# An mLSTM layer with an MLP: the order of its first steps written anew, and the last unit stored in two halves

## Chip, cores and metric

The kernel runs on one core of one Trainium2 chip. The metric is the device time of one execution in microseconds (us). The core has five engines with queues of their own: TensorE (PE, its weight loads PEld), VectorE (DVE), ScalarE (ACT), GpSimd (POOL) and SyncE (SP), which here issues nearly all DMA transfers.

## What is computed

Batch 4, 8 heads, 768 tokens, head size 40; then an MLP over the 3072 tokens with model size 320 and hidden size 2048. The recurrence, per head, with `C` a 40x40 state and `n` a vector:

```
m_new = max(f_t + m, i_t);  fs = exp(f_t + m - m_new);  is = exp(i_t - m_new)
C = fs*C + is * v k^T;      n = fs*n + is*k
y = sigmoid(o) * (C q) / max(|n.q|, 1)
out = silu(x @ w_in) @ w_out        # x = y with the heads side by side
```

w_in and w_out come as 64-bit floats, all else as 32-bit; the output is 32-bit.

## The kernel before

**Tiling.** The tokens are 24 units: 6 chunks of 128 tokens by 4 batch rows, unit n being chunk n // 4. A unit runs through the attention (two half chunks of 64 tokens, 8 heads as two sets of 4), which ends in a transposed x split into a rounded high part and a low rest. The MLP runs in an opening over units 0 to 3 and then in steps 1 to 10 of two units each. Hidden columns come in 16 groups of 128 (fc); a step takes two groups at a time (s = 0 to 7).

**Order.** Nothing is scheduled by the compiler: `ORDER` is a long list of words, and each word is one small step that puts its instructions at the end of the queues of the engines concerned. Every engine works its own list in order and waits by semaphores. SyncE too: a DMA issue that waits holds all DMA issues behind it. `V` and `Q` (and some `S`) also put an empty instruction on SyncE that waits for their matmuls.

**The words of a unit n:** `qk`, `kvo`, `lq`, `d` are its loads (L470, L479, L502, L490); `s`, `sp`, `sb` build the exponents of the first four units in PSUM by matmul (L526, L551, L564); `e` the exponential; `S` scores (L668, 32 matmuls); `w` scores times weights on DVE (L687); `v` weighted values on DVE (L605); `P` products for the state (L632); `c` the carry of the state (ACT copy, POOL and DVE); `l` the exponential of lq (ACT, L614), `q` the scaled queries (POOL, L618); `V` values (L697); `Q` queries against the state (L716, 16 matmuls for units 0 to 3, otherwise 32); `g` normalisation and output gate (five DVE steps, L733 to L743); `x` the transpose (L753 to L756); `h`, `y` high and low part (ACT, DVE).

**The gates of chunk c:** `gs`, `gu`, `gm`, `gt` on DVE, `gf` six small matmuls and a copy, and `go` the store of the summed forget gates to a DRAM scratch `LFd` (L276), from which `lq` and `d` are read.

**Weights.** w_in comes in 8 blocks `i` of 256 columns (256 rows) and 2 blocks `c` (the last 64 rows for four `i` blocks, L317), w_out in 8 blocks `o`. `L` loads one (L314), `M` (ACT, L329), `S`, `Z`, `J` (DVE, L337, L344, L357) turn 64-bit floats into 32-bit, `T` and `R` (ACT L381, DVE L386) split w_in into high and low part.

**MLP.** In the opening `m`, `a`, `b`, `n` with a letter A (units 0, 1), B (2, 3) or J (all four) and fc: first product (L780), tanh (L826), gate (L831), second product (L842 to L845). In a step j, `m`, `a`, `b`, `f`, `F`, `n` with j.s; the second product is L918. `On` copies unit n from PSUM (L929), `Dn` stores it (L799).

**Spins.** `z7*10` is ten matmuls of 128x512 bf16 on a constant into bank 7 (L939); they compute nothing that is used. The kernel has 39 of them, all before 16 us.

Of the kernel before, what the change touches and what calls it, by code (L numbers as in the profile page):

```python
# [49 lines left out]
ORDER = """  # L50
Li0 Li1 gs0 z2*5 z7*6 z7*6 gu0 kvo1 z7*2 z7*2 s0 Mi1 gm0 gt0 kvo0 gs1 s1 Si1 sp1 t1 z2*5 Mi0 Si0 Zi0 Zi1 sb1 Lc0 sp0 sb0
e0 gu1 e1 z7*10 gm1 Ji0 Mc0 Ti0 z7*1 v0 go0 qk1 lq0 S1 Sc0 gt1 qk0 z7*2 s3 Ji1 lq1 P0 Li3 qk2 lq2 Zc0 sb3 v1 Jc0 w1 t0
l0 c0 Ri0 S0 Tc0 Ti1 w0 sp3 l1 P1 Rc0 V0 gf1 q0 kvo2 Q0 s2 g0 Mi3 qk3 sp2 Si3 V1 q1 c1 sb2 e3 Zi3 Q1 g1 kvo3 S2 x0 lq3
e2 x1 l2 h0 h1 v2 w2 P2 Lo0 y0 Ri1 Li2 y1 q2 Lo1 t2 Ji3 V2 go1 c2 Lo3 mA0 v3 Q2 g2 S3 Lo2 t3 l3 P3 w3 aA0 mA1 c3 V3 bA0
aA1 x2 q3 Mo0 bA1 Q3 So0 h2 mA3 Zo0 mA2 y2 Jo0 Li4 Ti3 nA0 g3 Lc4 x3 nA1 Ri3 Mi2 d4 aA3 Mo1 bA3 So1 h3 y3 d5 aA2 mB0 bA2
Zo1 Jo1 Mo3 aB0 Si2 mJ6 Mi4 aJ6 bB0 Zi2 Ji2 nA3 gs2 lq4 Ti2 bJ6 mB2 qk4 nA2 kvo4 aB2 bB2 k5.0 So3 k4.1 nB0 Ri2 Mc4 Zo3
Jo3 Mo2 Li5 mJ7 k4.0 aJ7 mJ4 nJ6 aJ4 So2 bJ7 lq5 Sc4 qk5 Zo2 Si4 e4.0 e4.1 nJ7 mB3 bJ4 l4 Li6 aB3 Zc4 nB2 Zi4 v4 Ji4 Ti4
q4 mJ5 Jo2 S4.0 Lo5 Jc4 Mi5 Tc4 Lo4 bB3 Si5 P4 S4.1 gu2 aJ5 d6 Zi5 Ji5 Ti5 bJ5 nJ4 mB1 nJ5 k5.1 Ri4 Rc4 gm2 aB1 bB1 mJ9
aJ9 Ri5 mJ8 w4 bJ9 kvo5 Mo5 c4 e5.0 Mi6 Lo6 Mo4 So4 nB1 Si6 qk6 V4 e5.1 gt2 aJ8 Zo4 Li7 k6.1 l5 S5.0 t4 mJ10 bJ8 S5.1
Jo4 Q4 Zi6 Ji6 So5 nB3 Ti6 k6.0 nJ9 g4 nJ8 Ri6 Zo5 go2 e6.1 Mi7 v5 aJ10 kvo6 Si7 d7 mJ12 w5 Mo6 bJ10 Zi7 aJ12 Ji7 P5 V5  # L60
Jo5 Lo7 S6.0 q5 mJ13 c5 t5 So6 Q5 S6.1 e6.0 gl k7.0 aJ13 nJ10 bJ12 v6 mJ11 lq6 Ti7 aJ11 w6 Zo6 Mo7 x4 Jo6 bJ13 lq8 lq7
d8 Ri7 g5 nJ12 mJ14 h4 P6 k8.0 V6 y4 k7.1 bJ11 l6 l7 gf2 kvo7 e7.0 d9 mJ15 x5 uh0 So7 kvo8 qk7 h5 ul0 t6 Zo7 uh1 aJ14 y5
Jo7 nJ11 bJ14 nJ13 aJ15 q6 m1.0 bJ15 a1.0 ul1 nJ14 nJ15 b1.0 c6 m1.3 e7.1 gs3 uh3 q7 k9.0 f1.0 O0 ul3 O2 qk8 k9.1 m1.1
Q6 S7 uh2 O1 v7 ul2 O3 uh4 k8.1 a1.1 F1.0 e8.1 a1.3 g6 lq10 b1.3 P7 D2 n1.0 b1.1 f1.3 w7 m1.4 m1.6 f1.1 F1.3 ul4 F1.1
e8.0 lq9 x6 v8 a1.4 a1.6 b1.4 uh5 n1.3 n1.1 h6 e9.0 f1.4 m1.5 c7 b1.6 l8 gu3 y6 P8 F1.4 a1.5 kvo9 l9 V7 ul5 uh6 b1.5 D1
f1.6 q8 qk9 S8 t7 d10 w8 Q7 g7 c8 f1.5 e9.1 v9 kvo10 ul6 uh7 n1.4 m1.2 m1.7 F1.6 F1.5 lq11 x7 k10.1 n1.6 h7 a1.2 b1.2
qk10 y7 k10.0 P9 f1.2 D3 a1.7 V8 S9 gm3 Q8 b1.7 m2.1 F1.2 t10 w9 n1.5 m2.0 n1.2 a2.1 b2.1 f1.7 t9 m2.2 F1.7 a2.0 f2.1
ul7 b2.0 F2.1 gt3 n1.7 D0 t8 f2.0 a2.2 g8 qk11 O5 F2.0 b2.2 O4 m2.3 x8 f2.2 a2.3 go3 b2.3 e10.0 D4 h8 kvo11 t11 lq12
n2.0 m2.4 c9 e10.1 m2.5 q9 n2.1 F2.2 a2.4 b2.4 v10 d11 f2.3 m2.6 f2.4 y8 k11.1 F2.3 gf3 P10 F2.4 V9 S10 Q9 l10 w10 n2.2
# [34 lines left out]
def mlstm_mlp_kernel(  # L104
# [759 lines left out]
    class Step:
# [42 lines left out]
        def mm2(self, s):  # L907
            j = self.j
            gh, gl = self.g.pop(s)
            for k in range(FPS):  # L910
# [3 lines left out]
                ops = [(gh, hi), (gh, lo), (gl, hi)]
                for t in range(UPS):
                    ts = slice(k * NT + t * L, k * NT + (t + 1) * L)
                    for i, (g, w) in enumerate(ops):
                        nc.tensor.matmul(  # L918
                            self.po[t],
                            g[:, ts],  # L920
                            w,
                            start=(fc == 0 and i == 0),
                            stop=(last and i == len(ops) - 1),
                        )
# [145 lines left out]
```

## Time and profile before

| | us |
|---|---|
| median of 3 runs (lowest, highest) | 464.87 (463.38, 465.6) |
| profiled execution, device time | 465.92 |
| its span, first to last instruction | 464.1 |
| PE, PEld, DVE, ACT, POOL busy | 456.3, 423.5, 267.0, 208.8, 90.6 |

The span is what the profile sees between the first and the last instruction; the device time has 1.8 us around it. TensorE's clock is granted at one of two levels: 1.00 in the profile is 2.4 GHz, 0.50 is 1.2 GHz; the mean over the span is 0.971. In the profile's forty slices it is below 0.9 in the third and fourth only (23 to 46 us). A matmul's record overlaps that of the next, so the chain of waits, which counts each from the end of the one before, gives the time that one costs in a row of them.

### The profile page before, as it was taken

How to read it: one execution, taken by the hardware profiler on the slowest of the kernel's cores; microseconds unless marked ns; L12 is line 12 of the kernel's file. 1: busy time of each engine (PE TensorE's matmuls, PEld its weight loads, DVE VectorE, ACT ScalarE, POOL GpSimd, SP SyncE). 2: the span in 40 equal slices, each digit the busy share in tenths (PEclk: the TensorE clock that was granted, in tenths of full speed). 3: DMA queues.
4: the chain of work that ended last, by engine and by line, in shares of the span. 5: the costliest groups of instructions: out<-in, count | busy, mean ns of one | idle time of the engine just before them, and what ended most of it. 6: DMA issues, size and time to landing. Idle time of an engine off the chain costs nothing.

```text
span 464.1 us, 13697 instructions
## 1 busy us (share of the span) xinstructions
PE 456.3 (98%) x5849; PEld 423.5 (91%) x5849; DVE 267.0 (58%) x538; ACT 208.8 (45%) x485; POOL 90.6 (20%) x126
## 2 busy tenths in 40 slices
...
GB/s 254 187 167 213 273 78 238 140 127 134 43 89 158 57 94 96 16 82 111 2 123 150 46 87 163 17 82 99 51 127 96 1 81 74 2 30 1 30 0 30
DMA packets 25149, 44.63 MB, mean 96 GB/s; under 512 B 3264, under 2 KB 15488, under 8 KB 25088
## 3 DMA queue, kind: packets, MB, share of 16 engines
...
q14 instruction: 15, 0.12, 0.1%
...
## 4 chain that ended last, share of the span: by engine, by line
PE 94%; DMA 3%; DVE 1%; SPq 1%; issue 0%; POOL 0%; ACT 0%; DVEq 0%; ACTq 0%
PE psum L780 41%; PE psum L918 31%; PE psum L842 6%; PE psum L632 3%; PE psum L716 3%; PE psum L697 3%; PE psum L668 3%; PE psum L753 2%; DMA LFd<-G 2%; PE psum L844 1%; DMA lq<-LFd 1%; PE psum L845 1%; PE psum L756 1%; DMA G<-in_ig_dram 1%; SPq L502 0%
## 5 line engine op out<-in xcount | busy, mean ns | idle before, releaser
L918 PE MATMUL psum<-woh,g 128*128 128x320 f32 x640 | 153.0, 312 | 0.0
L918 PEld LDWEIGHTS psum<-woh,g 128*128 128x128 f32 x640 | 109.8, 188 | 0.2
L918 PE MATMUL psum<-wol,g 128*128 128x320 f32 x320 | 98.9, 309 | 0.0
L888 ACT ACTIVATE th<-psum 128x512 f32<-128x512 f32 x80 | 47.6, 596 | 106.3 <-PE psum L780 103.8
L892 DVE SCALAR_TENSOR_TENSOR th<-th,psum 128x512 f32<-128x512 f32 x80 | 54.4, 684 | 71.2 <-ACT th L888 70.8
L780 PE MATMUL psum<-xh,wh 128*128 128x256 f32 x480 | 85.4, 286 | 0.0
L780 PE MATMUL psum<-xl,wh 128*128 128x256 f32 x480 | 83.2, 282 | 0.0
L903 DVE TENSOR_TENSOR g<-th,g 128x512 fp32r<-128x512 f32 x80 | 60.2, 761 | 21.2 <-ACT g L899 20.4
L780 PEld LDWEIGHTS psum<-xh,wh 128*128 128x128 f32 x480 | 69.4, 188 | 1.0
L780 PEld LDWEIGHTS psum<-xl,wh 128*128 128x128 f32 x480 | 68.2, 188 | 0.0
L899 ACT CAST g<-th 128x512 fp32r<-128x512 f32 x80 | 48.9, 617 | 41.7 <-DVE th L892 26.8
L780 PE MATMUL psum<-xh,wl 128*128 128x256 f32 x320 | 64.1, 282 | 0.0
L918 PEld LDWEIGHTS psum<-wol,g 128*128 128x128 f32 x320 | 60.1, 188 | 0.0
L591 POOL TENSOR_SCALAR_AFFINE_SELECT D<-D 64x512 f32<-64x512 f32 x40 | 31.6, 791 | 93.1 <-DMA D<-LFd 73.6
L780 PEld LDWEIGHTS psum<-xh,wl 128*128 128x128 f32 x320 | 49.1, 188 | 0.0
L653 POOL TENSOR_TENSOR S<-S,eq 104x164 f32<-104x164 f32 x20 | 9.3, 466 | 180.6 <-DVE S L651 155.2
L585 ACT ACTIVATE D<-D,aT 128x64 f32<-128x64 f32 x160 | 42.1, 337 | 1.2 <-POOL D L591 1.2
L618 POOL TENSOR_TENSOR qt<-raw,eq 104x512 f32<-104x512 f32 x24 | 33.3, 1391 | 28.2 <-ACT eq L614 25.3
L780 PE MATMUL psum<-X,wh 128*128 128x512 f32 (+1 forms) x120 | 34.0, 403 | 0.0
L780 PEld LDWEIGHTS psum<-X,wh 128*128 128x128 f32 x120 | 22.7, 216 | 4.3
L687 DVE TENSOR_TENSOR D<-psum,D 128x512 f32<-128x512 f32 x24 | 16.5, 687 | 16.9 <-PE psum L668 16.8
L668 PE MATMUL psum<-raw 40*64 40x64 f32 x768 | 20.8, 230 | 1.2 <-DMA raw<-in_qk_dram 1.1
...
## 6 DMA issues: line engine op xcount, KB each, us to landing
kvo<-in_kvo_dram SPq DMA_DIRECT2D x24, 484.0 KB
...
wri<-in_w_in_dram SPq DMA_DIRECT2D x8, 512.0 KB
...
wrc<-in_w_in_dram SPq DMA_DIRECT2D x4, 256.0 KB
```

Source lines behind the costliest of these rows:

```text
L585: nc.scalar.activation(d[:, j, :], e[:, j, :], AF.Exp, bias=aT[:, self.c, hf, r : r + 1])
L591: nc.gpsimd.affine_select(out=d, in_=d, compare_op=ALU.is_ge, fill=NEG, base=0, pattern=[[0, H], [1, LB]], channel_multiplier=-1,)
L618: nc.gpsimd.tensor_tensor(out=self.qt, in0=self.q[:KP], in1=self.eq, op=ALU.mult)
L668: m = nc.tensor.matmul(self.ps[r * 64 : (r + 1) * 64, hf, j, :], self.k[rows, r ^ hf, j, :], self.q[rows, r ^ hf, j, :], start=True, stop= ...
L687: nc.vector.tensor_tensor(out=d, in0=self.ps, in1=d, op=ALU.mult)
L780: nc.tensor.matmul(ph, w, x, start=(i == 0), stop=(i == len(ops) - 1))
L842: nc.tensor.matmul(self.po[u][:, :DM], gs, w, start=(fc == 0), stop=last)
L888: nc.scalar.activation(th, self.ph[s], AF.Tanh, scale=0.5)
L892: nc.vector.scalar_tensor_tensor(out=th, in0=th, scalar=1.0, in1=ph, op0=ALU.add, op1=ALU.mult)
L899: nc.scalar.copy(t[:, 0], self.th[s])
L903: nc.vector.tensor_tensor(out=gl, in0=self.th.pop(s), in1=gh.bitcast(F32), op=ALU.subtract)
L918: nc.tensor.matmul(self.po[t], g[:, ts], w, start=(fc == 0 and i == 0), stop=(last and i == len(ops) - 1),)
```

## The change

Three edits:

- The first 20 or so lines of `ORDER`, up to the words of the third step, stand in another sequence. Every word other than the spins is there once in both; the spins go from 39 to 32, in other places.
- In the last second product (step 10, s = 7) the matmuls are sorted by unit, so that all of unit 22's come before all of unit 23's.
- Unit 23 is copied in two halves of 160 columns, the first by ScalarE and the second by VectorE, and stored by two DMAs, the first issued by ScalarE and the second by SyncE.

```diff
 ORDER = """
-Li0 Li1 gs0 z2*5 z7*6 z7*6 gu0 kvo1 z7*2 z7*2 s0 Mi1 gm0 gt0 kvo0 gs1 s1 Si1 sp1 t1 z2*5 Mi0 Si0 Zi0 Zi1 sb1 Lc0 sp0 sb0
-e0 gu1 e1 z7*10 gm1 Ji0 Mc0 Ti0 z7*1 v0 go0 qk1 lq0 S1 Sc0 gt1 qk0 z7*2 s3 Ji1 lq1 P0 Li3 qk2 lq2 Zc0 sb3 v1 Jc0 w1 t0
-l0 c0 Ri0 S0 Tc0 Ti1 w0 sp3 l1 P1 Rc0 V0 gf1 q0 kvo2 Q0 s2 g0 Mi3 qk3 sp2 Si3 V1 q1 c1 sb2 e3 Zi3 Q1 g1 kvo3 S2 x0 lq3
-e2 x1 l2 h0 h1 v2 w2 P2 Lo0 y0 Ri1 Li2 y1 q2 Lo1 t2 Ji3 V2 go1 c2 Lo3 mA0 v3 Q2 g2 S3 Lo2 t3 l3 P3 w3 aA0 mA1 c3 V3 bA0
-aA1 x2 q3 Mo0 bA1 Q3 So0 h2 mA3 Zo0 mA2 y2 Jo0 Li4 Ti3 nA0 g3 Lc4 x3 nA1 Ri3 Mi2 d4 aA3 Mo1 bA3 So1 h3 y3 d5 aA2 mB0 bA2
...
+z7*4 gs0 gu0 Li0 gm0 Lc0 Li1 s0 gs1 gu1 s1 Mc0 Mi0 gm1 z7*11 Mi1 Sc0 go0 qk0 gt0 kvo0 sp0 Zc0 gt1 Si1 Jc0 sb0 sp1 Tc0
+sb1 e0 Si0 lq0 l0 Zi1 t0 S0 e1 kvo1 Rc0 z7*10 Zi0 z7*5 Ji0 lq1 v0 qk1 s2 l1 Ji1 s3 lq2 sp2 sp3 q0 P0 v1 sb3 kvo2 w0 gf1
+qk2 c0 Ti0 V0 S1 Q0 sb2 t1 Lo0 Ri0 w1 P1 g0 q1 e2 v2 e3 kvo3 c1 Ti1 l2 V1 z2*2 qk3 Q1 g1 x0 h0 S2 Mo0 Lo1 P2 w2 Ri1 x1
+h1 V2 y0 y1 q2 So0 mA0 mA2 c2 lq3 aA0 Li3 Q2 Zo0 v3 S3 t2 go1 bA0 aA2 Mo1 bA2 w3 Lo3 mA3 P3 aA3 g2 Jo0 Li2 Lc4 So1 l3
+Zo1 bA3 Li4 V3 Jo1 x2 d4 t3 q3 h2 nA0 lq4 y2 Mi3 mA1 Si3 c3 Mo3 Lo2 Q3 aA1 nA3 g3 Mi2 nA2 bA1 x3 Zi3 nA1 h3 Ji3 y3 Li5
+d5 Ti3 qk4 Si2 mB0 aB0 Ri3 Zi2 bB0 mJ7 Ji2 So3 aJ7 Ti2 bJ7 Ri2 mJ6 Mc4 Zo3 aJ6 mB3 Mi4 nB0 bJ6 mB1 k4.0 kvo4 aB3 k4.1
...
@@ sent @@
-        nc.sync.dma_start(out[b * S + c * L : b * S + (c + 1) * L, :], obs.pop(n))
+        rows, ob = out[b * S + c * L : b * S + (c + 1) * L, :], obs.pop(n)
+        if n == NU - 1:
+            nc.scalar.dma_start(rows[:, : DM // 2], ob[:, : DM // 2])
+            nc.sync.dma_start(rows[:, DM // 2 :], ob[:, DM // 2 :])
+        else:
+            nc.sync.dma_start(rows, ob)
@@ Step.mm2 @@
-            for k in range(FPS):
+            pairs = [(k, t) for k in range(FPS) for t in range(UPS)]
+            if j == NSTEP - 1 and s == NSL - 1:
+                pairs.sort(key=lambda p: p[1])
+            for k, t in pairs:
...
@@ Step.copy @@
-            nc.scalar.activation(ob, self.po[t], AF.Copy, scale=0.5)
+            half = DM // 2 if n == NU - 1 else DM
+            nc.scalar.activation(ob[:, :half], self.po[t][:, :half], AF.Copy, scale=0.5)
+            if half < DM:
+                nc.vector.tensor_scalar(ob[:, half:], self.po[t][:, half:], 0.5, None, op0=ALU.mult)
```

## Rows read from the trace of the kernel before

**Rows 1.** Windows view: busy time of the engines, granted clock and DMA by stretch.
```profile
core 0: us, PE busy (x) PEld busy (x) DVE busy (x) ACT busy (x) POOL busy (x), PEclk, DMA share, GB/s
4.00:12.00 8.00, 8.00 (x122) 4.15 (x121) 4.70 (x14) 2.78 (x5) 2.33 (x5) 1.00 0.93 298
12.00:21.00 9.00, 7.63 (x223) 4.96 (x220) 8.10 (x16) 4.86 (x9) 2.97 (x3) 1.00 0.57 169
21.00:22.50 1.50, 0.00 (x0) 0.03 (x1) 1.01 (x2) 0.66 (x1) 0.36 (x1) 0.50 0.92 273
22.50:34.00 11.50, 11.49 (x218) 8.80 (x218) 7.45 (x19) 3.24 (x7) 1.73 (x2) 0.50 0.54 160
34.00:44.80 10.80, 10.56 (x154) 8.97 (x150) 5.55 (x14) 3.87 (x10) 2.17 (x3) 0.50 0.69 250
44.80:48.20 3.40, 3.40 (x18) 3.40 (x17) 3.28 (x10) 1.72 (x4) 0.00 (x0) 0.50 0.58 178
50.00:130.00 80.00, 79.41 (x805) 64.42 (x805) 59.77 (x111) 40.18 (x96) 22.19 (x23) 1.00 0.46 142
130.00:461.00 331.00, 330.94 (x4307) 326.38 (x4305) 176.33 (x353) 149.53 (x354) 55.67 (x73) 1.00 0.23 68
```
**Rows 2.** TensorE: three lines of its timeline, then of the chain: start, us.
```profile
10.77 2.58 PE L939 MATMUL psum<-G 128*128 128x512 bf16 x11
14.55 0.61 PE L939 MATMUL psum<-G 128*128 128x512 bf16 x2
22.50 1.08 PE L716 MATMUL psum<-S,qt 40*64 40x41 f32 x16 [1.72 <-issue]
...
32.21 1.02 PE psum L632 x32
34.09 2.01 PE psum L780 x8
39.33 2.01 PE psum L780 x8
42.36 0.62 PE psum L753 x2
43.81 1.01 PE psum L716 x16
44.83 3.66 PE psum L780 x16
55.41 0.95 PE psum L780 x8
93.95 0.61 PE psum L632 x32
```
**Rows 3.** Chain that ended last, before the first queries: start, us, what.
```profile
5.48 7.04 DMA LFd<-G
15.32 3.96 DMA lq<-LFd
20.10 1.28 POOL qt L618
21.37 1.13 issue
22.50 1.08 PE psum L716 x16
```
**Rows 4.** DMA view: issues by tensor; then the instruction queue, 19 to 21 us.
```profile
kvo<-in_kvo_dram SPq DMA_DIRECT2D x24, 484.0 KB
wri<-in_w_in_dram SPq DMA_DIRECT2D x8, 512.0 KB
wrc<-in_w_in_dram SPq DMA_DIRECT2D x4, 256.0 KB
...
q8 instruction: 1, 0.02, 4.0%
```
**Rows 5.** Timelines of ScalarE (three lines) and VectorE (one): start, us, what.
```profile
7.29 0.68 ACT L329 ACTIVATE wti<-wri 128x512 f32<-128x512 f32 x1 [4.60 <-DMA wri<-in_w_in_dram]
10.91 1.09 ACT L575 ACTIVATE D<-psum 128x512 f32<-128x512 f32 x2 [1.36 <-PE psum L564]
16.75 1.26 ACT L381 CAST wh<-wtc 64x512 fp32r<-64x512 f32 x2
...
13.06 0.48 DVE L605 TENSOR_TENSOR vw<-kvo,D 128x328 f32<-128x328 f32 x1
```
**Rows 6.** The last copies (timeline), and copies by shape: busy us, mean ns.
```profile
460.54 0.88 ACT L929 ACTIVATE ob<-psum 128x320 f32<-128x320 f32 x2 [4.22 <-PE psum L918]
...
L861 ACT ACTIVATE ob<-psum 128x192 f32<-128x192 f32 x1 | 0.3, 332 | 0.0
L861 ACT ACTIVATE ob<-psum 128x128 f32<-128x128 f32 x1 | 0.3, 288 | 0.0
```

More of the change, by code (lines that the diff above doesn't have):

```diff
@@ L56 @@
[L56 to L65, printed above, removed]
@@ L66 @@
-f1.6 q8 qk9 S8 t7 d10 w8 Q7 g7 c8 f1.5 e9.1 v9 kvo10 ul6 uh7 n1.4 m1.2 m1.7 F1.6 F1.5 lq11 x7 k10.1 n1.6 h7 a1.2 b1.2
+z7*4 gs0 gu0 Li0 gm0 Lc0 Li1 s0 gs1 gu1 s1 Mc0 Mi0 gm1 z7*11 Mi1 Sc0 go0 qk0 gt0 kvo0 sp0 Zc0 gt1 Si1 Jc0 sb0 sp1 Tc0
+sb1 e0 Si0 lq0 l0 Zi1 t0 S0 e1 kvo1 Rc0 z7*10 Zi0 z7*5 Ji0 lq1 v0 qk1 s2 l1 Ji1 s3 lq2 sp2 sp3 q0 P0 v1 sb3 kvo2 w0 gf1
+qk2 c0 Ti0 V0 S1 Q0 sb2 t1 Lo0 Ri0 w1 P1 g0 q1 e2 v2 e3 kvo3 c1 Ti1 l2 V1 z2*2 qk3 Q1 g1 x0 h0 S2 Mo0 Lo1 P2 w2 Ri1 x1
+h1 V2 y0 y1 q2 So0 mA0 mA2 c2 lq3 aA0 Li3 Q2 Zo0 v3 S3 t2 go1 bA0 aA2 Mo1 bA2 w3 Lo3 mA3 P3 aA3 g2 Jo0 Li2 Lc4 So1 l3
@@ new lines @@
+Zo1 bA3 Li4 V3 Jo1 x2 d4 t3 q3 h2 nA0 lq4 y2 Mi3 mA1 Si3 c3 Mo3 Lo2 Q3 aA1 nA3 g3 Mi2 nA2 bA1 x3 Zi3 nA1 h3 Ji3 y3 Li5
+d5 Ti3 qk4 Si2 mB0 aB0 Ri3 Zi2 bB0 mJ7 Ji2 So3 aJ7 Ti2 bJ7 Ri2 mJ6 Mc4 Zo3 aJ6 mB3 Mi4 nB0 bJ6 mB1 k4.0 kvo4 aB3 k4.1
+bB3 Sc4 Jo3 Li6 aB1 bB1 Zc4 e4.1 Lo4 mJ5 Jc4 e4.0 mJ4 d6 Tc4 Lo5 Rc4 nJ7 gs2 k5.0 Mo2 nB3 aJ4 k5.1 nB1 bJ4 So2 aJ5 nJ6
+Si4 Zo2 Mi5 bJ5 Zi4 Si5 Jo2 Ji4 mB2 S4.0 v4 Mi6 aB2 P4 Ti4 gu2 Ri4 Li7 S4.1 Mo4 k6.1 nJ5 bB2 mJ8 Si6 w4 nJ4 Zi5 So4 l4
+aJ8 mJ9 qk5 kvo5 Zo4 Jo4 Zi6 kvo6 bJ8 lq5 Mo5 nJ8 S5.0 V4 q4 So5 Ji5 Ti5 d7 Ri5 aJ9 mJ10 e5.0 e5.1 bJ9 c4 Mi7 k7.0 t4
```

27 lines of the change are left out of this document (16 added, 11 removed).

## Prediction

> **What bounds the kernel now.** I read the windows view first, then the chain of waits, then each engine's own timeline. From 130 to 461 us TensorE is busy 330.94 of 331 us at a granted clock of 1.00 (2.4 GHz), and from 50 to 130 us 79.41 of 80 [rows 1]. Nothing in the changed stretch makes that work shorter, since every word of the old order except the spins is in the new one once. So the end moves by what the first 50 us lose: by the time at which TensorE has done a given amount of its work.
>
> Two things are lost there. One is the clock: it is at 0.50 (1.2 GHz) from 21.0 to 48.2 us, while TensorE is busy 11.49 + 10.56 + 3.40 = 25.45 of 25.7 us after 22.5 [rows 1]. The same products of a unit take 1.02 us there and 0.61 later, a first product of the MLP 2.01 and 0.95 [rows 2]. These 25.45 us would be about 13 at full clock. The other is the chain in front of it: the first query matmuls (Q0) start at 22.5 us, and the chain back from them is the gate store to DRAM (5.48 us, landing 7.04 later), the load lq0 (15.32, 3.96 to land), the exponential, the scaling of q on GpSimd, and 1.13 us in which TensorE waits for nothing that is shown [rows 3].
>
> **The change part by part.**
>
> *The gate store goes up.* Before, go0 is issued at 5.48 behind two blocks of w_in (512 KB each), two kvo (484 each), the two halves of a wrc (256 each) and the gates (144): 2,648 KB [rows 4]. In the new order both kvo stand behind it: 968 KB less. At the 298 GB/s that moved from 4 to 12 us [rows 1] this is 3.3 us, so the store lands at about 9.2, not 12.5. lq0 is SyncE's next but two (qk0 and kvo0 are issued before it and don't wait), so it lands at about 13. SyncE waits at lq0 for the store; queued behind that wait are kvo1, lq1, qk1, lq2, kvo2 and qk2, now issued from about 10.5 on, where kvo1 went at 2.2 before. They are wanted by v1, S1 and v2, at 16 us and later: free by about 3 us.
>
> *wrc first on ScalarE and VectorE.* Mc0 now heads ScalarE, and Sc0 stands before gt0 on VectorE, so gt0, gt1, the key matmuls, e0 and all behind them wait for the landing of wrc, at the place in the queue where the second w_in block landed before, 7.3 us [rows 5]. From there: Mc0 to 8.0, Sc0, gt0, Zc0, gt1 on VectorE to 9.7, Mi1, Si1 and Jc0 to 10.8, the two casts Tc0 (1.26) to 12.1, e0 (0.55) to 12.7; before, both exponentials began at 10.91 [rows 5]. Then Rc0, Zi0 and Ji0 on VectorE, so v0 at about 15.0, where the first v stood at 13.06. This is 1.5 to 2 us given away.
>
> *Spins.* 39 become 32, but 15 of them now stand between S0 and s2. Eleven take 2.58 us [rows 2], so 15 take 3.5. raw0 lands after 2,000 KB, at about 10.8; S0 0.6, spins to 14.9, then s2, s3, sp2, sp3 to 16.5, against v0 at 15.0: P0 comes 1.4 us later by them. P0, sb3, gf1, V0 and S1 are 0.5 to 0.6 each, so Q0 starts at about 19.6. At Q0 both orders have done the same kinds and, within one unit's keys and products, the same number of matmuls. Bounds for Q0: 17.5 (all landings early, the spins covered) to 22.5 (as before). What is late at Q0 is then TensorE's own list, no longer lq0 (whose qt is ready at about 15).
>
> The 1.13 us of unexplained waiting before Q0 [rows 3] comes while the DMA engines are 0.92 busy [rows 1], and a page of instructions is among what they move from 19 to 21 us [rows 4]. If it is TensorE's and came late, the new order, which puts other matmuls there, may or may not lose it: zero to 1.1, inside the bounds of Q0. The Trainium skill (Runtime: NRT & Kernel Launch, section "Instruction fetch mechanics") calls the crossing of a block mostly hidden; by it, minding the pages gives nothing, by the row 1.1 us at most.
>
> *From Q0 to the first MLP matmuls.* Before, the last spins ran until 15.1 us and the clock fell at 21.0, after a stretch of products, values, scores and spans with hardly a gap (7.63 of 9.0 us busy from 12 to 21) [rows 1, 2]. The new order ends its spins at about 14.9 and then issues the same kinds, so I let the clock fall at 21 again; its two later spins (0.45 us at most, and they must wait for the bank that w1 reads) I give no effect. Between Q0 and mA0 stand sb2, P1, V1, two spins, Q1, x0, S2, P2, x1, V2: 5.6 us at full clock by 0.6 for a group of 32, 0.3 for Q1 and 0.7 for a transpose (half of the 1.45 from 42.36 to 43.81 [rows 2]); at 1.02 to 0.61 they take 9.4. mA0 starts at 29 to 29.5. VectorE's chain alone (each gate step 1.5, w, Ri1, y0, y1) would reach mA0 at 26.7, so it is hidden by the slow clock, and becomes the bound if the clock holds.
>
> *The clock's rise.* Single first products at 34.09 and 39.33 did not raise the clock; it rose at 48.2, at the end of 3.66 us of two adjacent ones [rows 1, 2]. The old order has its first such pair (mA3 mA2) after all four units; the new one has mA0 mA2 adjacent right after V2: 4.0 us at 1.2 GHz, so the rise comes at about 33.5. What the old order has done at 48.3 and the new one has not at 33.5 is S3, P3, V3 (0.6 each), Q2, Q3 (0.3 each), x2 (0.7), mA1 and mA3 (0.95 each): 5.0 us at full clock. Gain: 48.3 - 33.5 - 5.0 = 9.8.
>
> *Given back.* VectorE was idle 25.7 - (7.45 + 5.55 + 3.28) = 9.4 us between 22.5 and 48.2, and busy 75% from 50 to 130 [rows 1]. The gain takes most of that idle time, so some weight blocks will be late: I charge 1 us, between 0 and 5.
>
> *The last unit.* Sorting the last second product by unit ends unit 22 three matmuls sooner (0.44 us), so its copy and store no longer stand with the last one's. The last copy is 0.44 us of ScalarE for 320 columns; 192 take 0.33 and 128 take 0.29 [rows 6], so 160 take 0.31 beside VectorE's half, which is idle. Both stores now go at once, about 0.44 apart from unit 22's: 0.1 to 0.4 off the transfer. I take 0.5 in all; bounds are 0.2 lost (a store issued from ScalarE behind its own copy, rows of half the length) and 0.9 won.
>
> Sum: -9.8 + 1.0 - 0.5 = -9.3. The profiled execution took 465.92 us (span 464.1), so 456.6; the median of the runs shown is 1.05 under it: **455.6**.
>
> **The rivals.**
>
> *The clock holds through to the MLP.* For it: the fall at 21.0 is at the start of the 1.72 us idle before Q0 [rows 1, 2], which the new order may not have. Against: 20.8 is when that idle begins, so it is hardly what was answered by a fall 0.2 us later. Then VectorE's chain sets mA0 at 26.7, the pair ends at 28.6, the gain is 14.7, less 2 for VectorE, plus 0.5: 451.7. The Trainium skill (TensorE: Matmul & The Clock Gate, section "Why this matters for your kernels") lays drops to idle gaps between bursts and would speak for this; the rows speak against it.
>
> *The pair does not raise the clock.* It stands at another place in time, and 2.01 us of such work did not do. The next adjacent ones are nA0 mA1, after 3.75 us of other work (6.9 at half clock): their end is at 44.7, where the old order would be at 49.1. Gain 4.4, less 1, plus 0.5: 461.0.
>
> *Weights late.* The clock recovers, but mB0 or mJ7 wait for the blocks of w_in that VectorE and the queue can't deliver 10 us sooner (DMA share 0.69 from 34 to 44.8 [rows 1]): 5 us lost for 1, so 459.6.
>
> *Slower: the half clock lasts past the opening's first products.* The new order cuts the MLP's runs by Q2, S3, P3, V3, x2, Q3 and x3. If none of them but mJ7 raises the clock, 7.1 us more of work run at half speed, to 58.8 us, where the old order would be at 56.1: 2.7 lost, 0.5 won at the tail: 467.1. It decides from a rise later than about 55 us. Against: runs of 4 us that are longer than the one that raised it.
>
> *It does nothing:* Q0 and the rise both slide along with some landing: 464.5.
>
> **How the numbers follow.** The forecast 0.48, its own range 453 to 458.5; the clock holds 0.17; the pair fails 0.13; weights late 0.10; slower 0.08; nothing 0.04. A change under 0.5% (2.3 us) can't be told from none here. Faster by more: the forecast, the clock that holds, and most of the next two: 0.82. Within: 0.10. Slower: 0.08. The range 450.5 to 463 leaves out the last two cases (0.12) and the ends of the bounds of the others.
>
> **What would show it.** Right: the first LFd store landing near 9 us, Q0 under 21, granted clock 0.50 from about 21 to about 34, the span ending near 455. Wrong: a fall before 17 or a rise after 42; TensorE idle before mB0 or mJ7 waiting for VectorE or w_in; the end more than 3.2 us behind the last matmul.

## The result: 0.6% slower, and the profile after

The change makes the kernel slower. The median is 465.64 us over 15 runs (464.56 to 467.55); the kernel before, run beside it 15 times, has 463.38 us (460.26 to 466.42). The ratio, here one of mean times, is 1.006, with a 95% interval of 1.0031 to 1.0089 (the two medians alone would give 1.0049). The prediction was 455.6 us and faster. Medians, low-clock times and offsets below count every execution; the ratios leave out those over 1.5% above the fastest of their kernel (8 of the old kernel's, 4 of 12 with the clock held up in the old order, one each in two others).

The profiled execution took 464.56 us: span 462.8, mean granted clock 0.978. Of the forty slices of its page the second, third and fourth have the clock below 0.9:

```profile
PEclk9857999999999999999999999999999999999999
```

The windows view of the kernel after, first two of the stretches of [rows 1], then four that follow its clock and show two low stretches, where before there was one:

```profile
22.50:34.00 11.50, 9.21 (x164) 6.42 (x162) 5.26 (x15) 3.54 (x8) 2.07 (x2) 0.50 0.56 185
50.00:130.00 80.00, 80.00 (x819) 65.39 (x818) 61.45 (x117) 42.26 (x100) 19.70 (x22) 1.00 0.52 152
...
12.00:20.20 8.20, 7.69 (x210) 5.25 (x208) 6.94 (x12) 4.05 (x9) 3.71 (x4) 0.99 0.82 226
20.20:37.20 17.00, 14.71 (x223) 11.00 (x222) 8.30 (x22) 4.86 (x11) 2.54 (x3) 0.50 0.45 140
37.20:43.97 6.77, 5.36 (x132) 4.39 (x132) 4.53 (x11) 2.83 (x7) 1.27 (x1) 1.00 0.57 184
43.97:47.40 3.43, 3.43 (x12) 2.63 (x10) 2.88 (x6) 1.73 (x4) 1.06 (x1) 0.50 1.06 292
```

The clock falls at 20.1, rises at 37.2, falls again at 44.0 and rises at 47.4 us: 20.4 us at half clock against 27.2 before [rows 1]. TensorE, which hardly stopped before from 22.5 to 34 us (11.49 of 11.50), is now idle for 2.29 us of it.

TensorE's timeline of the kernel after (start, us, line, operation; idle time before it and what ended it in brackets), which answers to [rows 2]:

```profile
19.84 1.16 PE L716 MATMUL psum<-S,qt 40*64 40x41 f32 x16
20.94 1.13 PE L564 MATMUL psum<-minus,G 16*64 16x256 f32 x8
21.99 1.09 PE L632 MATMUL psum<-vw,kvo 64*64 64x41 f32 x32
24.57 0.43 PE L697 MATMUL psum<-kvo,D 64*64 64x41 f32 x2 [1.49 <-ACT S L648]
25.81 1.08 PE L697 MATMUL psum<-kvo,D 64*64 64x41 f32 x30 [0.80 <-DVE S L654]
26.82 1.04 PE L948 MATMUL psum<-G 128*128 128x512 bf16 x2
...
34.62 1.01 PE L780 MATMUL psum<-X,wh 128*128 128x256 f32 x3
...
41.80 0.68 PE L697 MATMUL psum<-kvo,D 64*64 64x41 f32 x32 [1.08 <-DVE x L740]
42.80 0.44 PE L753 MATMUL psum<-ident,x 128*128 128x128 f32 x2 [0.33 <-DVE x L743]
```

Three groups wait. V1 (24.57) waits for the carry c1: first for its copy on ScalarE, then, two matmuls on, for its sum on VectorE. V3 (41.80) waits for VectorE's gate step, and x2 (42.80) for another. The timelines of ScalarE and VectorE show c1's two ends; the copy itself is held up 1.01 us by VectorE's gate step (L740), which reads the same PSUM bank, and that step starts only when P1 (L632) is done:

```profile
24.23 0.30 ACT L648 COPY S<-psum 104x164 f32<-104x164 f32 x1 [1.01 <-DVE x L740]
...
23.18 0.17 DVE L733 TENSOR_SCALAR nq<-psum 128x8 f32<-128x8 f32 x1 [2.43 <-PE psum L632]
23.70 0.44 DVE L740 SCALAR_TENSOR_TENSOR x<-kvo,psum 128x320 f32<-128x320 f32 x1
25.43 0.33 DVE L654 TENSOR_TENSOR S<-S,psum 104x164 f32<-104x164 f32 x1 [0.35 <-POOL S L653]
```

The end of the kernel after, in order of time, answers to [rows 6]. Unit 22's copy and store are out of the way, but the halves of unit 23 don't run beside each other: VectorE's starts 0.34 us after ScalarE's, just as that ends.

```profile
459.11 0.33 SPq L804 DMA_DIRECT2D out_dram<-ob  x1
459.18 0.31 PE L924 MATMUL psum<-woh,g 128*128 128x320 f32 x1
459.53 0.30 ACT L936 ACTIVATE ob<-psum 128x160 f32<-128x160 f32 x1 [0.44 <-PE psum L924]
459.87 0.33 DVE L938 TENSOR_SCALAR ob<-psum 128x160 f32<-128x160 f32 x1 [4.27 <-ACT ob L936]
460.22 0.33 SPq L802 DMA_DIRECT2D out_dram<-ob  x1
```

### The profile page after: what moved, and what is told of

It reads as the page before. It is cut to its first block, busy times and chain, and to the rows that moved or that the text cites. A ratio compares the mean times of both kernels' runs of the same rounds, so it can differ in the third digit from the quotient of the medians.

```text
span 462.8 us, 13682 instructions
## 1 busy us (share of the span) xinstructions
PE 453.3 (98%) x5842; PEld 420.0 (91%) x5842; DVE 265.8 (57%) x539; ACT 209.7 (45%) x485; POOL 89.5 (19%) x126
## 4 chain that ended last, share of the span: by engine, by line
PE 97%; issue 2%; DVE 1%; POOL 0%; ACT 0%; POOLq 0%
PE psum L780 41%; PE psum L924 31%; PE psum L847 6%; PE psum L668 3%; PE psum L632 3%; PE psum L716 3%; PE psum L697 2%; PE psum L948 2%; PE psum L753 2%; PE psum L849 1%; PE psum L850 1%; PE psum L756 1%; PE psum L551 0%; PE psum L526 0%; PE psum L260 0%
## 5 line engine op out<-in xcount | busy, mean ns | idle before, releaser
L653 POOL TENSOR_TENSOR S<-S,eq 104x164 f32<-104x164 f32 x20 | 10.2, 511 | 159.4 <-DVE S L651 141.3
L618 POOL TENSOR_TENSOR qt<-raw,eq 104x512 f32<-104x512 f32 x24 | 31.7, 1323 | 39.1 <-ACT eq L614 38.7
L780 PE MATMUL psum<-X,wh 128*128 128x512 f32 (+1 forms) x120 | 32.2, 388 | 0.0
L687 DVE TENSOR_TENSOR D<-psum,D 128x512 f32<-128x512 f32 x24 | 16.5, 687 | 19.2 <-PE psum L668 19.2
L780 PEld LDWEIGHTS psum<-X,wh 128*128 128x128 f32 x120 | 21.6, 206 | 4.3 <-issue 0.6
L697 PE MATMUL psum<-kvo,D 64*64 64x41 f32 x768 | 17.8, 234 | 3.7 <-ACT S L648 1.5
```

The costliest lines, as they stand in the source:

```text
L618: nc.gpsimd.tensor_tensor(out=self.qt, in0=self.q[:KP], in1=self.eq, op=ALU.mult)
L687: nc.vector.tensor_tensor(out=d, in0=self.ps, in1=d, op=ALU.mult)
L697: m = nc.tensor.matmul(self.po[k * 64 : (k + 1) * 64, hf * HF + j, :], self.Dm[rs, h, :], self.vt[rs, h, :], start=(j == 0), stop=(self.c ...
L780: nc.tensor.matmul(ph, w, x, start=(i == 0), stop=(i == len(ops) - 1))
```

## Experiments

Two numbers stand with each run beside the ratio. The *low-clock time* of an execution is 2 x (1 - mean granted clock) x span, since the clock has two levels. The *offset* is how far a kernel's executions lie, in the mean, above a line through the 180 listed executions of the old kernel (those alike in time, span and clock taken once, 165): time = 454.3 + 0.39 x low-clock time, all in us (0.6 us scatter about it). It tells "slower at the same clock" from "slower because the clock was low longer". Both are worked out from the listed runs, and both have limits. The clock before its first recorded rise isn't in the mean clock (more on this below). Within the executions of thirteen kernels with the new order the slope is 0.355 +- 0.012, so that offsets of two kernels that differ by 9 us of low-clock time can be off by 0.3. And the runs were made in six groups, each with the old kernel beside it, whose own executions lie between -0.3 and +0.2 of the line by group: a difference of 0.4 between offsets of different groups decides nothing.

**The kernel before, once more.**

> The kernel before, unchanged, once more, to see the granted clock of each of its runs beside its time. If its spread from 460.3 to 466.4 us comes from how long the clock stands at 1.2 GHz, time and mean clock go together: runs near 460.5 have a mean clock near 0.98, those near 465 near 0.971, about 0.5 us of time for each us at the low level. If it comes from something else (a landing, an instruction page), runs of one clock differ by several us.

Median 463.9, ratio 0.9995 (0.9962 to 1.0029). Its executions spread from 461.1 to 465.7 us, and in order of their clock: those at 0.971 took 464.8 to 465.7, at 0.981 461.1 to 461.7. Over all runs the old order had 11 to 31 us at low clock, 23.0 in the mean, and 458.6 to 468.0 us. The profile that I predicted from had 26.9: it was one of the longer ones.

**The two edits apart.** One kernel has the old `ORDER` with the new end, the other the new `ORDER` with the old end.

```diff
-pairs.sort(key=lambda p: p[1])       # new_order_old_end: also one copy, one store
...
-z7*4 gs0 gu0 Li0 gm0 ...             # old_order_new_end: ORDER of before
+Li0 Li1 gs0 z2*5 z7*6 ...
```

> The old order with the last unit in two halves. By the prediction the end is 0.5 us shorter, so about 0.5 under the kernel before. By the two profiles the end is not shorter at all (3.30 us from the last matmul to the end of the span, 3.14 before), since VectorE's half starts only when ScalarE's is done (459.87 against 459.53): then 0 to 0.2 longer.

> The new order with the last unit in one piece. If the slowdown is the order's, this is as slow as the changed kernel or 0.2 us faster, about 465.5. If the end were the cause, it would come to the kernel before, about 463.4, or by the forecast's own working under it.

The new end alone: 464.06, ratio 1.0018 (0.9976 to 1.0059), offset +0.12 +- 0.19. The new order alone: 465.31, ratio 1.0025 (0.9995 to 1.0056, by time alone not clear of none), offset +2.48 +- 0.16 with 21.2 us at low clock; the whole change has +2.60 +- 0.19 and 23.0. So the loss is the order's, 2.5 us at equal clock, and its gain at the clock, which I put at 9.8, isn't there: 23.0 us against 23.0. The new end is worth nothing that these runs can tell from none.

**The carry behind V1.** c1 is moved so that its copy no longer stands in front of V1.

```diff
-... kvo3 c1 Ti1 l2 V1 z2*2 qk3 ...
+... kvo3 Ti1 l2 V1 c1 z2*2 qk3 ...
```

> The changed kernel with one word moved: the carry of unit 1 (c1) behind the values of unit 1 (V1), where the old order has it. Theory 1: V1 stood 1.49 + 0.80 us waiting for the carry's ScalarE copy and its VectorE sum, and the whole way to the first MLP product came later by it; V1 is done by about 24.2, mA0 starts at about 32.5 instead of 34.6, the time falls by about 2 us to 463.5. Theory 2: the clock alone sets the time, and 2 us sooner only moves the same work within the low clock: the rise stays where it was, and the time changes by under 1 us.

464.62, ratio 1.0054 (1.0026 to 1.0082), offset +1.77 +- 0.22, low clock 21.4 us. TensorE's timeline of this kernel shows why so little came back:

```profile
26.74 1.09 PE L697 MATMUL psum<-kvo,D 64*64 64x41 f32 x32 [1.08 <-DVE x L740]
```

V1 now waits 1.08 us for VectorE's gate step of unit 0 (g0), which reads the bank that V1 writes. In the kernel after, this wait lay hidden under the 1.49 us for c1.

**Two of unit 2's steps behind Q0.** The kernel above, and s2 and sp2 where VectorE is still busy with g0.

```diff
-... qk1 s2 l1 Ji1 s3 lq2 sp2 sp3 q0 ... Q0 sb2 ... c1 Ti1 l2 V1 z2*2
+... qk1 l1 Ji1 s3 lq2 sp3 q0 ... Q0 s2 sp2 sb2 ... Ti1 l2 V1 c1 z2*2
```

> The new order with c1 behind V1 and with s2 and sp2 moved behind Q0, where the old order has them: V1 must wait until VectorE has read Q0's result out of the shared bank, and these two (1.9 us at 1.2 GHz) then stand in that wait. If that wait (1.08 us with c1 moved alone) is a loss: 1 us under the kernel with c1 moved alone, about 463.6. If the clock alone decides, the same as that kernel, 464.6.

465.4, ratio 1.0048 (1.0018 to 1.0077), offset +2.14 +- 0.15, low clock 22.9. The expectation missed: V1 still waits 1.08 us. VectorE's timeline says why:

```profile
24.83 0.17 DVE L733 TENSOR_SCALAR nq<-psum 128x8 f32<-128x8 f32 x1 [3.43 <-PE psum L632]
25.35 0.43 DVE L740 SCALAR_TENSOR_TENSOR x<-kvo,psum 128x320 f32<-128x320 f32 x1
```

g0 doesn't begin when Q0 is done (at 21.4) but when P1 is (L632, at 24.8), the group right in front of V1. What is moved to between Q0 and P1 shifts P1, g0 and V1 alike. The old order has P1 ahead of Q0 and V1 two groups behind it. Putting P1 back there is tried below.

**Without the 15 spins behind S0.**

```diff
-... kvo1 Rc0 z7*10 Zi0 z7*5 Ji0 lq1 v0 ...
+... kvo1 Rc0 Zi0 Ji0 lq1 v0 ...
```

> The new order without the 15 spins between S0 and s2. By the prediction's own reckoning Q0 comes 1.4 us sooner (P0 then waits for v0 only). [...] If they hold the clock up where it matters, the time is 1.5 to 3 us longer.

467.4, ratio 1.0085 (1.0054 to 1.0116). The offset falls to +0.62 +- 0.13, so the spins cost about 2.0 us at equal clock; but low-clock time rises to 31.9 us, and these 8.9 us more cost more. Windows and timeline of this kernel:

```profile
15.36 0.64 PE L526 MATMUL psum<-past,one 32*64 32x256 bf16 x8 [2.04 <-ACT D L575]
...
12.00:20.00 8.00, 5.28 (x122) 4.02 (x121) 5.53 (x8) 3.90 (x9) 2.77 (x4) 0.50 0.70 229
20.00:42.00 22.00, 19.55 (x316) 15.40 (x320) 10.02 (x26) 5.74 (x13) 3.42 (x4) 0.50 0.41 130
```

s2 waits for e1 instead, and the clock is low from before 12 us to 42. The 1.5 to 3 us more that I had expected for spins that hold the clock up came: the time is 1.8 us above the 465.64 of the change. With the new order's own slope (0.355) the spins' price at equal clock is 1.7.

**The clock held up by force.** Both orders with spins of half the width (128x256) in threes in front of the small groups up to x2: 57 in the old order, 54 in the new one (there with c1 behind V1 and without the two spins z2).

```diff
-... kvo2 Q0 s2 ... Si3 V1 ... Zi3 Q1 ...
+... kvo2 hold1*6 Q0 hold1*3 s2 ... Si3 hold5*3 V1 ... Zi3 hold1*3 Q1 ...
```

> The old order with 57 spins of half length (128x256) set in threes between TensorE's groups of small matmuls from S0 (unit 0) to Q3 (six before Q0), to keep the clock at 2.4 GHz through the front. They add 57 x 0.107 = 6.1 us of TensorE time at full clock, part of it in waits. Theory 1, the low clock (some 23 us of it in a mean run) is what the front loses: the clock stays at 1.00 or nearly, 23 us of half clock give back 10 to 11 us, and the time comes to about 457 to 459. Theory 2, at full clock the chain of VectorE, ScalarE and the transfers sets the pace: the clock holds too, but TensorE waits, and the time stays within 2 us of 463.3.

> The new order with c1 behind V1, without its two spins z2*2, and with 54 spins of 128x256 in threes from sp2 to x2. Theory 1 (the low clock is the price): 456 to 460, as the spins add 5.8 us and the clock gives back 10. Theory 2 (waits of V1, V3 and x2 for VectorE set the pace at full clock): 462 to 465.

The old order: 465.06, from 461.8 to 472.2 (463.06 without the four longest), ratio 1.0005 (0.9966 to 1.0045); the new: 463.46, ratio 1.0029 (0.9991 to 1.0068). The clock does hold, with 9.6 and 5.0 us at low clock in the mean, and in the profile of the old one it is at full speed from 20 to 50 us, with TensorE idle for only 0.82:

```profile
20.00:50.00 30.00, 29.18 (x494) 22.07 (x487) 21.98 (x53) 11.72 (x26) 4.33 (x7) 1.00 0.70 222
22.07 0.84 PE L946 MATMUL psum<-G 128*128 128x256 bf16 x6
23.44 0.51 PE L946 MATMUL psum<-G 128*128 128x256 bf16 x3
```

But both have an offset of 8.0 to 8.2. Three spins more cost 0.33 us (0.84 - 0.51), so 57 cost about 6.3 where they stand on the path: they eat what they win. Of the old order's offset 1.9 us more stay without a cause. The profile also shows that VectorE doesn't stop the attention of four units from running at full clock.

**Spins only where TensorE waits.** In the new order 11 half-width spins before V1 and 6 before V3; in the old one 14 before Q0, where it had been idle 1.72 us [rows 2].

```diff
-... Ti1 l2 V1 ... Li4 V3 ...           # fill_new
+... Ti1 l2 hold1*11 V1 ... Li4 hold1*6 V3 ...
...
-... kvo2 Q0 ...                        # fill_old
+... kvo2 hold1*14 Q0 ...
```

> The changed kernel with 11 spins of 128x256 put before V1 and 6 before V3, into waits that TensorE has there anyway (1.49 + 0.80 us for the carry at V1, 1.08 for VectorE at V3). At 1.2 GHz 11 take 2.35 us, so they cost nothing or 0.2 us if the waits stay. [...] Theory 2 (the waits matter only because they let the clock lie low): the clock comes up by the spins at V1, low-clock time under 15 us, and the time is under 462.

> The old order with 14 spins of 128x256 (1.5 us at 2.4 GHz) before Q0, in the wait of 1.4 to 1.7 us that TensorE has there. [...] If the wait was not what let the clock fall, the same as before or up to 0.5 us longer.

In the new order this beats both kernels: 460.79 us, ratio 0.9951 (0.9922 to 0.998). Its offset is that of the change (+2.56 +- 0.16), but its low-clock time is 10.5 us in place of 23.0. In the old order it costs: 467.1, ratio 1.0087 (1.0055 to 1.0118), offset +2.40 +- 0.13, low clock 26.0; I had expected 0.5 us more at most.

**Only the 11 spins before V1.**

```diff
-... Ti1 l2 V1 ...
+... Ti1 l2 hold1*11 V1 ...
```

> The changed kernel with the 11 spins of 128x256 in the wait before V1 alone; the wait before V3 stays empty. If the wait at V1 is what lets the clock lie low through to the first MLP products, nearly all of the gain is here: low-clock time 10 to 13 us, the time 460.8 to 462. If the second fall (at 44 us in the changed kernel, after the waits of V3 and x2) is a cost of its own, it comes back: low-clock time about 14 us, 462 to 463.

461.28, ratio 0.9978 (0.994 to 1.0015), low clock 13.4, offset +2.44 +- 0.13. So the spins before V1 do most of it, and the six before V3 may add a little (10.5 against 13.4). Its timeline and windows, beside those of the old order with 14 spins, show what the spins do. First the new order, where the clock falls at 20.1 as in the kernel after:

```profile
23.86 2.53 PE L955 MATMUL psum<-G 128*128 128x256 bf16 x11
26.32 1.12 PE L697 MATMUL psum<-kvo,D 64*64 64x41 f32 x32
...
20.20:26.90 6.70, 6.70 (x110) 4.77 (x105) 3.19 (x9) 2.43 (x5) 1.21 (x2) 0.50 0.41 132
27.00:50.00 23.00, 20.79 (x349) 16.29 (x346) 18.33 (x42) 9.42 (x20) 5.39 (x6) 1.00 0.84 250
```

Then the old one:

```profile
22.66 3.17 PE L946 MATMUL psum<-G 128*128 128x256 bf16 x14 [0.41 <-issue]
...
26.20:29.50 3.30, 2.69 (x94) 1.95 (x92) 1.99 (x8) 1.14 (x3) 0.46 (x1) 1.00 0.31 99
29.60:50.00 20.40, 20.15 (x283) 16.95 (x284) 13.74 (x34) 7.27 (x17) 3.43 (x4) 0.50 0.65 215
```

In both the spins come after the fall, and the clock rises right behind them, at about 27 and 26 us. In the new order, where they stand in a wait that is there anyway, the clock then stays up. In the old one it falls again at 29.5, and its 3.17 us of spins take the place of 1.72 us of idle time. Why one stays up and the other falls isn't settled. It isn't idle time: the new order keeps full clock from 27 to 50 us with TensorE idle for 2.21, and the old one is at half clock from 29.6 to 50 us with 0.25 idle.

**VectorE's half in a buffer of its own** (old order, new end, a single execution), to see whether the two halves stood in line because of the shared output tile.

```diff
+o2 = p2.tile([128, DM], F32, tag="vw", name="o2")[:, :half]
-nc.vector.tensor_scalar(ob[:, half:], self.po[t][:, half:], 0.5, None, op0=ALU.mult)
+nc.vector.tensor_scalar(o2, self.po[t][:, half:], 0.5, None, op0=ALU.mult)
```

> The old order with the last unit in two halves, VectorE's half written to a buffer of its own. If VectorE's half waits for ScalarE's because both write one buffer, it now starts with it, about 0.35 us sooner, and the end from last matmul to the end of the span is near 3.0 us instead of 3.3. If it waits because both read one PSUM tile, it starts as late as before.

461.08 us, which at its clock (0.981) is the old kernel's time. The copies still run in turn:

```profile
456.02 0.30 ACT L936 ACTIVATE ob<-psum 128x160 f32<-128x160 f32 x1 [0.44 <-PE psum L924]
456.36 0.33 DVE L939 TENSOR_SCALAR o<-psum 128x160 f32<-128x160 f32 x1 [4.27 <-ACT ob L936]
```

What they still share is the PSUM tile that both read; no run has the halves in two tiles of PSUM, so that this is the cause is argued, not shown.

After these runs two parts of the 2.5 us at equal clock were suspected: the waits of V1, and the clock's first rise. The records of the clock begin as it first rises, at 3.9 to 6.7 us in the six profiles of old-order kernels (5.5 in the mean) and at 6.4 to 9.2 in the eight of new-order ones (7.9); the new order has 4 spins ahead of its first real matmuls, the old one 21. The views print 1.00 for the time before, but there is no record of it: in the kernel after the first 4 spins take 1.89 us, where 15 later ones at full clock take 3.45. Four runs were made for these.

**P1 ahead of V0**, with c1 behind V1.

```diff
-... c0 Ti0 V0 S1 Q0 sb2 ... w1 P1 g0 q1 ... kvo3 c1 Ti1 l2 V1 z2*2 ...
+... c0 Ti0 P1 V0 S1 Q0 sb2 ... w1 g0 q1 ... kvo3 Ti1 l2 V1 c1 z2*2 ...
```

> The changed kernel with P1 in front of V0, where the old order has it, and c1 behind V1. If V1 waits because VectorE's gate step g0 starts only behind P1, which now stood right in front of V1: g0 starts behind Q0, V1's waits (2.29 us in the changed kernel, 1.08 with c1 moved) go under 0.5, the offset at equal clock falls from 1.85 (c1 moved alone) to about 0.8, and the median from 464.6 to about 463.6. Rival, that another dependence takes the wait's place (P1 ahead of V0 waits for the carry c0 itself): V0 or Q0 come as much later as V1 gains, and it stays at 464.6, offset 1.9.

463.31, ratio 0.9995 (0.9961 to 1.003): the loss is gone. Timelines of VectorE and TensorE:

```profile
21.73 0.16 DVE L733 TENSOR_SCALAR nq<-psum 128x8 f32<-128x8 f32 x1
...
22.73 0.68 PE L697 MATMUL psum<-kvo,D 64*64 64x41 f32 x32 [0.63 <-DVE x L740]
24.57 0.28 PE L716 MATMUL psum<-S,qt 40*64 40x41 f32 x2 [0.62 <-issue]
25.42 0.66 PE L716 MATMUL psum<-S,qt 40*64 40x41 f32 x14 [0.58 <-DVE S L654]
```

g0 starts without a wait of its own and V1 waits 0.63 us, though Q1 now waits 1.2. The mechanism is right and its price isn't: the offset stays at +2.15 +- 0.19 (0.8 was expected), and what falls is the low-clock time, from 23.0 to 16.5 us. At 0.39 each this is 2.5 us, most of what was won.

**The first spins in one piece**, in the change and in the kernel above.

```diff
-z7*4 gs0 gu0 Li0 gm0 Lc0 Li1 s0 gs1 gu1 s1 Mc0 Mi0 gm1 z7*11 Mi1 ...
+z7*15 gs0 gu0 Li0 gm0 Lc0 Li1 s0 gs1 gu1 s1 Mc0 Mi0 gm1 Mi1 ...
```

> The changed kernel with its first two groups of spins (4 and 11) in one piece ahead of s0 and s1. If the clock's later first rise (7.9 us in the mean of eight profiles of the new order, 5.5 in six of the old) is a part of the offset of 2.7 us: the first spins show a rise near 5.5 us, the offset falls by about 1.2 to 1.5, the median to about 464.4. Rival, that the first microseconds are covered (TensorE waits later in the opening for ScalarE's and VectorE's chain anyway): offset 2.7, median 465.6, whatever the rise.

> The two kernels above together. If both are separate parts of the offset, they add up: offset about 0 (-0.5 to 0.5), and with 21 to 23 us at low clock a median near 462.5. If both only open another wait: as the better of the two, about 463.6 or more.

The change with it: 466.7, ratio 1.0064 (1.0032 to 1.0096), offset +2.44 +- 0.19. The clock first rises at 5.7 us, and nothing is won. TensorE's timeline shows the cover that I had doubted: the group behind now waits 1.36 us, where the change waits 0.81.

```profile
0.93 5.76 PE L948 MATMUL psum<-G 128*128 128x512 bf16 x15 [0.93 <-DVE warm L999]
...
9.08 1.13 PE L564 MATMUL psum<-minus,G 16*64 16x256 f32 x8 [1.36 <-issue]
```

With P1 ahead as well: 464.27, ratio 1.0004 (0.9967 to 1.0042), offset +2.51 +- 0.14, low clock 17.6. In neither does the offset fall.

**The same with the spins in the waits** (11 before V1, 6 before V3).

> The version with 11 spins before V1 and 6 before V3, with the first spins in one piece too. If the first rise is a part of the offset and the clock behind it stays as it was: offset 1.5 in place of 2.7, median about 459.6. Rival, that the first rise is covered: 460.8. Should another place of the first spins shift the later rises and falls, the low-clock time moves from 10.5 us, at 0.40 us each.

461.37, ratio 0.996 (0.9927 to 0.9992), offset +2.65 +- 0.11, low clock 12.0: ahead of both kernels, but the rival again, no better than without the one piece.

**Ten of the 15 spins**, in the version with spins in the waits.

```diff
-... z7*10 Zi0 z7*5 Ji0 lq1 v0 ...
+... z7*10 Zi0 Ji0 lq1 v0 ...
```

> The version with 11 spins before V1 and 6 before V3, with 10 of the 15 spins behind S0. If the offset of 2.7 us is mostly these spins' own time (15 cost 2.0): offset 1.9 to 2.1; with low-clock time still near 10.5 us a median of 460.1, and if the clock falls earlier without them, as much slower as 0.40 us for each us. Rival, that the offset is something else and the 15 spins only fill a wait for the exponential: offset 2.7, median 460.8 or, with more low clock, above.

460.4, ratio 0.9946 (0.9911 to 0.9981), the third version that beats both kernels; low clock 11.6, offset +2.21 +- 0.23. Against +2.56 +- 0.16 with 15 spins that is 0.35 less, of the expected sign and within what the runs scatter. The two runs are of different groups, though: against the old kernel beside each they are +2.87 and +2.12, and the 0.75 between them is what was expected (0.6 to 0.8). So it speaks for a price of the spins, and doesn't decide it.

**P1 ahead, and spins in the waits that are left**: six before Q1, six before V3.

```diff
-... kvo3 Ti1 l2 V1 c1 z2*2 qk3 Q1 ... Li4 V3 ...        # P1_ahead
+... kvo3 Ti1 l2 V1 c1 z2*2 qk3 hold1*6 Q1 ... Li4 hold1*6 V3 ...
```

> P1 ahead of V0, c1 behind V1, six half-width spins in front of Q1 (where it waits 1.2 us with P1 ahead) and six in front of V3. If both gains add: low-clock time falls from 16.5 to about 8 us at an offset of 2.2, median 460. Rival, that what held the clock was the 11 dense spins in one place after the fall, and not the missing waits: low clock stays near 16, and the spins on the path cost up to 0.5: 463.3 to 463.8.

460.62, ratio 0.9963 (0.9923 to 1.0004), low clock 10.2 (16.5 without these spins), offset +2.56 +- 0.12. The two gains add nearly as forecast, but the sum is what the spins alone had reached. Its profile has the shortest span of all (457.4 us), and the clock doesn't fall once from 20 to 50 us, although TensorE is idle for 3.06 of these 30:

```profile
20.00:50.00 30.00, 26.94 (x495) 20.86 (x496) 23.49 (x54) 12.33 (x27) 7.72 (x9) 1.00 0.80 235
```

## Why the prediction was wrong

| step of the prediction | predicted | after |
|---|---|---|
| gate store lands, lq0 issued | 9.2 | 9.33 |
| exponential e0 starts | 12.1 | 12.18 |
| v0 | 15.0 | 15.56 |
| Q0 starts | 19.6 | 19.84 |
| clock falls | 21 | 20.1 |
| mA0 starts | 29 to 29.5 | 34.62 |
| clock rises, with mA0 mA2 | 33.5 | 37.2 |
| second fall | none | 44.0 to 47.4 |
| last matmul to end of span, change | -0.5 | +0.1 |
| profiled execution | 456.6 | 464.56 |

The rows of the kernel after for the first lines of it:

```profile
9.33 0.69 SPq L502 DMA_DIRECT2D lq<-LFd  x2
...
12.18 0.60 ACT L575 ACTIVATE D<-psum 128x512 f32<-128x512 f32 x1
...
15.56 0.49 DVE L605 TENSOR_TENSOR vw<-kvo,D 128x328 f32<-128x328 f32 x1
```

**What was right.** All steps up to Q0, within 0.6 us (the 1.13 us of unexplained waiting in front of it didn't come back), and that the clock rises with the pair mA0 mA2: in all eight profiles of the new order without spins in the waits of V1, Q1 and V3 (the change, its old end, c1 behind V1, s2 behind Q0, without the 15 spins, P1 ahead, and the two with the first spins in one piece and nothing in the waits) it rose within that pair or at most 0.7 us behind it, between 34.0 and 42.0 us.

**The step that failed: from Q0 to the first MLP matmuls.** I priced it at 9.4 us; it took 14.8 (34.62 - 19.84). The 5.4 us are 2.29 of V1's waits, 1.0 for the two spins z2, to which I gave no effect, and about 2.1 of mis-sized groups: Q0's own 1.10 (to 20.94) wasn't in my list, Q1 stood with 0.5 (0.3 at full clock) where 16 such matmuls take 1.01 at half clock [rows 2], the two transposes took 0.6 and the six groups of small matmuls 0.5 more than I had. Against that, the list adds up to 5.3 us at full clock, not to the 5.6 that I wrote, which is 0.5 at half clock. I had worked out VectorE's chain and found it hidden "by the slow clock"; the waits came through PSUM instead: the new order puts P1 between Q0 and V1, g0 doesn't start before P1 ends, and c1's copy and V1 wait for g0 to have read the bank. My sum had durations and no such chain.

**The gain at the rise, 9.8, was 5.4, and was given back.** The pair ends at 37.9, so 48.3 - 37.9 - 5.0 = 5.4. The second fall, which I didn't foresee, takes 1.7 (3.43 us busy at half clock), the waits of V3 and x2 1.4 (I had 1.0 given back to VectorE); that leaves 2.3. The last matmul starts 1.45 us earlier (459.18, before 460.63), so 0.9 has to be found. At unit 9's gate step (178 us) the new order is still 1.96 ahead, at unit 10's (199 us) 1.45: 0.5 goes in between, probably at 177 us, where TensorE stands between two matmuls of the MLP for a cause that the profile doesn't name. The other 0.4 stays without a place. Less 0.1 at the end, the two profiled executions differ by 1.36. The row of the stand at 177 us:

```profile
177.26 0.41 PE L924 MATMUL psum<-wol,g 128*128 128x320 f32 x1 [0.24 <-issue]
```

**The base was one execution's clock.** I took the stretch from 21.0 to 48.2 us for a property of the old order. It is one draw: 26.9 us at low clock by its mean clock, where the mean of 165 executions is 23.0, worth 1.5 us by the line above; the profiled execution of the change had 20.4 where its mean is 23.0, worth 1.0.

In the old order the rise is such a draw too. I argued from [rows 2] that one first product doesn't raise the clock and an adjacent pair does. There it rose at 48.3 and 47.4 us in two profiles, but at 40.9 (with the new end) and 35.7 (with two tiles) in others, both times right behind a single product, mA1 and mA0. The latter:

```profile
33.50 1.01 PE L780 MATMUL psum<-X,wh 128*128 128x256 f32 x3
...
18.70:35.60 16.90, 16.90 (x322) 13.65 (x315) 10.22 (x25) 5.72 (x12) 4.29 (x5) 0.50 0.65 206
35.80:50.00 14.20, 13.55 (x189) 11.08 (x186) 12.29 (x29) 7.36 (x15) 2.20 (x3) 1.00 0.81 259
```

So the old order doesn't always have to wait for its pair. And what the new order wins at the rise it loses in two places that weren't in my sum. In five of the eight profiles named above the clock falls before 17 us, which I had named as a sign of being wrong; in none of the six of old-order kernels does it fall before 18. And in five of the eight it falls again at 43 to 47 us. Windows of the new order with the old end show both:

```profile
11.30:14.60 3.30, 2.96 (x35) 1.62 (x33) 3.17 (x5) 2.39 (x5) 0.10 (x1) 0.50 0.79 219
45.50:48.70 3.20, 3.20 (x11) 2.42 (x10) 2.87 (x6) 1.71 (x4) 1.06 (x1) 0.50 1.06 316
```

Why the clock falls there stays open. In the mean the change wins nothing at the clock, and the 1.36 us of the two profiles turn round; what they leave of the 2.26 between the medians is within the scatter of single executions. The experiments *same* and the two edits apart show this.

**What the 2.5 us at equal clock are** is settled only in part. Most of them aren't V1's waits (P1 ahead: 2.15; c1 behind V1: 1.77), nor the first rise (first spins in one piece: 2.44), nor the end (0.12). The 15 spins behind S0 are the one part that a run shows: without them the offset is 0.62. I had counted them only as 1.4 us that P0 comes later, inside a Q0 that came at the time forecast. That leaves the price at 1.7 to 2.0, and the run with ten of them agrees only against its own old kernel; what the rest is stays open.

**How the waits hurt.** Mostly through the clock. With P1 ahead, or with spins in the waits, the offset falls by 0.5 at most and the low-clock time falls from 23.0 to 16.5 or 10.5 us. With either, the new order is level with the old or ahead of it.

**The rivals.** That the clock holds was wrong, and the price I gave it (451.7) as well: held by force it wins nothing, though the spins' own 6.3 us are in that, and the one execution with few added spins (P1 ahead, 12 spins) whose clock is recorded at 1.00 throughout took 457.27. Weights weren't late: from 50 to 130 us TensorE is busy 80.00 of 80. The slower rival had the right sign and the wrong mechanism; the rise came at 37.2, long before the 55 us from which it was to decide. On the Trainium skill's rule that I weighed (TensorE: Matmul & The Clock Gate, section "Why this matters for your kernels": drops come from idle gaps between bursts), the runs disagree for this kernel: in the kernel after the clock fell with no gap over 0.3 us in the 6 us before, in the old order with 14 spins it was down with TensorE 20.15 of 20.40 us busy, and with two of unit 2's steps behind Q0 it fell once more far inside the MLP, after 16.00 us of 16.00 busy. That with P1 ahead and 12 spins it stayed up through 3.06 us of idle time in 30 says less, since these are several short waits. The windows view of the fall inside the MLP:

```profile
176.50:179.80 3.30, 3.30 (x26) 3.22 (x18) 2.58 (x8) 0.00 (x0) 0.00 (x0) 0.50 0.24 76
```

**The last unit.** I took 0.5 off because VectorE is idle. It is, but its half waits for ScalarE's, so the second store is issued one copy later. A rule of the Trainium skill that I hadn't weighed bears on it (PSUM — Partial Sum Buffer, section "PSUM bank collisions raise a hardware error"): the program has to keep two engines out of one bank and the same partitions at a time, two readers too. The trace agrees: VectorE's half starts 0.34 us after ScalarE's, which takes 0.30, whatever the output buffer. What it is worth: +0.12 +- 0.15 at equal clock, by a joint fit of the kernel before, the change and its two edits apart.
